# Linformer attention with a maxout FFN on one core: the last batch's softmax sums leave TensorE, and batch 0's first quarter of q is loaded as fp32

## The chip, the cores and the metric

The kernel runs on one core of one Trainium2 chip. The metric is the device time of one execution in microseconds (us). A profile of one execution, with a trace of every instruction and DMA packet, lies beside the times. In the trace PE is TensorE (PEld its weight loads), DVE is VectorE, ACT is ScalarE, POOL is GpSimd, and SP is the engine whose queue issues most DMAs.

## The reference, cut to what matters

```python
# q, k, v: (8, 8, 1024, 64) = batch, head, position, head_dim; E, F: (64, 1024)
k_proj = np.einsum('ks,bhsd->bhkd', E, k)          # 64 keys per head
v_proj = np.einsum('ks,bhsd->bhkd', F, v)
scores = scale * np.matmul(q, k_proj.transpose(0, 1, 3, 2))
attn = np.exp(scores - scores.max(-1, keepdims=True))
attn = attn / (attn.sum(-1, keepdims=True) + 1e-09)
attn_out = np.matmul(attn, v_proj)
x = attn_out.transpose(0, 2, 1, 3).reshape(8 * 1024, 512)
h = np.maximum(np.maximum(x @ w1, x @ w2), x @ w3)  # w1, w2, w3: (512, 768)
out = h @ w_out                                     # w_out: (768, 512)
```

All tensors are fp32 in memory. The kernel computes in bf16 with fp32 accumulation and takes the exponentials without subtracting the maximum.

## The kernel before, in words

**Stages.** The kernel works through eight batches. The FFN of batch b is the main stream: for each of two chunks (`ch`) of 512 positions there are six up steps (`up`, one per 128 columns of the hidden layer: 3 weight matrices times 4 contraction tiles, 12 matmuls of 512 columns) and four down steps (`down`, 6 matmuls of 512 columns for 128 positions). In an up step ACT copies the first product to SBUF (`h1s`), and VectorE takes two maxima (`m12`, then `hT`). In a down step of batches 1 to 7 ACT copies the result (`o_sb`), and every second down step a 512 KB store goes out on SP's queue.

**Order.** The order on every engine is written by hand: `tc.manual_schedule` keeps program order, and Tile adds the semaphores. The attention of batch b+1 is slipped in behind single steps of batch b's FFN. `plan(b)` (L830) is a table from (chunk, step) to functions, where steps 0 to 5 are the up steps and 6 to 9 the down steps; `behind` runs the entry after the step. PSUM banks are dealt by `bank` and `two` from a clock model (`runs`, `pe`, `free`) that is kept while the program is written; it sets which bank is used, not the order.

**Attention of a later batch.** `qd` packs q and turns it by DMA to `qT`; `kvproj` or `kproj`/`vproj` make the projected keys and values; `sc(b, g)` computes the scores of the head pair g with the keys on the partitions (two halves of the positions on partitions 0 to 63 and 64 to 127) and ACT writes their exponentials, the softmax numerators, as bf16 into `pTs[b, g, 0]`. `zc(b)` (L256) then sums the numerators of all four head pairs over the keys with eight matmuls against the constant `pick`, takes the reciprocal on ACT as exp(-ln), writes it to a DRAM scratch `zd`, and reads it back four times with a broadcast over 64 partitions into `zi_all`. `vx(b, g)` (L291) multiplies numerators by projected values on TensorE (`values`, four 64x64 tiles) and VectorE scales the product with `zi_all` into `xT`, the input of batch b's up steps. For the last batch, b = 7, `zc` stands behind up step 3 of chunk 0 of batch 6, and `vx` behind steps (1, 2) and (1, 6) of batch 6.

**The start.** E and F come on SP's queue (L148, L149). q, k, v and the weights of the start come on POOL's queue, which turns fp32 into bf16 on the way (`load_q`, `load_kv`, `load_w`); the first is q of heads 0 to 3 for the first half of each partition's positions (L167). Batch 0's first 512 positions are then worked off in an order of their own (L652 to L682): TensorE runs 512-column fp32 matmuls on zeros (`idle`) to stay busy, `turn_ef` casts E and F to bf16 on VectorE and ACT, turns them on TensorE and copies them to `efT`; `q_duo(0)` turns q with 16 transposes, and VectorE copies them to `qT`; then a VectorE copy doubles one part of `efT`, one more `idle`, and `k_duo(0)` (L593) projects the first four heads' keys.

Of the kernel before, what the change touches and what calls it, by code (L numbers as in the profile page):

```python
# [8 lines left out]
FP32 = mybir.dt.float32  # L9
BF16 = mybir.dt.bfloat16  # L10
AF = mybir.ActivationFunctionType
ALU = mybir.AluOpType
# [3 lines left out]
def kernel(  # L16
# [13 lines left out]
    nc = tc.nc  # L30

    B, H, S, D = q.shape
# [5 lines left out]
    P = 128  # L38
    HALF = 64
    SI = 8  # L40
    NCT = DM // P
    NJT = DF // P
    NPAIR = H // 2
    CHUNK = 512
    NCHUNK = S // CHUNK
    SPC = SI // NCHUNK
# [5 lines left out]
    att = ctx.enter_context(tc.tile_pool(name="att", bufs=2))  # L52
    scratch = ctx.enter_context(
        tc.tile_pool(name="scratch", bufs=2, space=bass.MemoryType.DRAM)
    )
# [21 lines left out]
    def two():  # L77
        n = min(range(0, 8, 2), key=lambda n: max(free[n:n + 2]))
        deal((n, n + 1))
        return psum_t[:, n:n + 2, :], (n, n + 1)  # L80

    def bank():
        n = min(range(8), key=lambda n: free[n])
        deal((n,))
        return psum_t[:, n, :], (n,)

    def pe(dt, wait=0.0):
        clock["pe"] = max(clock["pe"], wait) + dt
        return clock["pe"]

    def runs(eng, ready, dt, ns=()):
        if eng in clock:
            clock[eng] = max(clock[eng], ready + 0.06) + dt
            for n in ns:
                free[n] = clock[eng]
            return clock[eng]
        return ready + dt
# [3 lines left out]
    def copy(eng, o, i, ns=(), dt=0.65):  # L101
        done = {  # L102
            "v": nc.vector.tensor_copy, "s": nc.scalar.copy, "g": nc.gpsimd.tensor_copy
        }[eng](out=o, in_=i)
        runs(eng, clock["pe"] if ns else 0.0, dt, ns)
        return done
# [10 lines left out]
    def view(src, b):  # L117
        return src[b].rearrange("h (p si) d -> p h si d", si=SI)


    ident = const.tile([P, P], BF16, name="ident")
# [9 lines left out]
    qkv, qTs, kpTs, vps, pTs, zis, xTs = {}, {}, {}, {}, {}, {}, {}  # L131
# [24 lines left out]
    def load_q(heads, sis):  # L156
        nc.gpsimd.dma_start(
            out=q_t[:, heads, sis], in_=view(q, 0)[:, heads, sis]
        )
# [4 lines left out]

    LO, HI, ALL = slice(0, H // 2), slice(H // 2, H), slice(0, H)
    V2, V3 = slice(4, 6), slice(6, 8)
    load_q(LO, slice(0, SPC))  # L167
    load_kv(1, LO)
    load_q(HI, slice(0, SPC))
    load_kv(1, HI)  # L170
# [80 lines left out]
    def zi_all(b):  # L251
        if b not in zi_alls:
            zi_alls[b] = att.tile([P, NPAIR, 2, CHUNK], FP32, name="zi_all", bufs=1)
        return zi_alls[b]

    def zc(b, queue=nc.sync):  # L256
# [31 lines left out]
                zis[b, g, 0] = zi_all(b)[:, g], when  # L288
        return f

    def vx(b, g):  # L291
        def f():
            scale_x(b, g, 0, SI, values(b, g, 0, SI))
        return f
# [75 lines left out]

    q_pk = {}

    def pack_q(b, gs, lo, nsi):


        def f():
            if b not in q_pk:
                q_pk[b] = att.tile([P, NPAIR, SI, 2, D], BF16, name="q_p", bufs=1)
            for g in gs:
                copy(  # L380
                    "s", q_pk[b][:, g, lo:lo + nsi].rearrange("p si h d -> p h si d"),
                    qkv[b][0][:, 2 * g:2 * g + 2, lo:lo + nsi], (), 0.58,
                )
        return f

# [184 lines left out]
    def turn_ef():  # L570
        for i in range(2):
            cols = slice(i * S // 2, (i + 1) * S // 2)
            copy("vs"[i], ef_b[:, cols], ef_f[:, cols])
        t, ns = two()
        t = t.bitcast(BF16)[:, 0]
        src = ef_b.rearrange("k (p si) -> k p si", si=SI)
        for si in range(SI):
            nc.tensor.transpose(
                out=t[:, si * P:(si + 1) * P], in_=src[:, :, si], identity=ident
            )  # L580
        pe(0.6)
        for i in range(2):
            copy(
                "vs"[i], efT[:, 4 * i:4 * i + 4, 0:P],
                t[:, i * CHUNK:(i + 1) * CHUNK].rearrange("p (si x) -> p si x", x=P), ns,
            )
# [46 lines left out]
    def q_duo(u):  # L633
        t, ns = bank()
        t = t.bitcast(BF16)
        for gg in range(2):
            heads_q(0, 2 * u + gg, range(SPC), t[:, gg * CHUNK:(gg + 1) * CHUNK])
        o = qTs[0].rearrange("a (g si) p -> a g si p", si=SI)
        copy(
            "v", o[:, 2 * u:2 * u + 2, 0:SPC, :],  # L640
            t.rearrange("a (g si p) -> a g si p", si=SPC, p=P), ns, 0.7,
        )

    C0 = (0, SPC)

    def z(g):
# [5 lines left out]
    idle(3, warm_f)  # L652
    at(6.3)
    turn_ef()
    q_duo(0)
    copy("v", efT[:, :, P:P + KP], efT[:, :, KP:P])
    idle(1, warm_f)
    at(9.0)
# [22 lines left out]
    v_pair(1)  # L681
    at(17.4)  # L682

    ffn_sb = ctx.enter_context(tc.tile_pool(name="ffn_sb", bufs=2))
    hTs = {}

    def up_mm(h, i, b, ch, jt, cts, first=0, last=NCT - 1):
# [14 lines left out]
    def up_first(work):  # L702


        def then(key):
            run_later()
            for f in work.get(key, []):
                f()

        hs = ffn_sb.tile([P, NJT, CHUNK], FP32, name="hs", bufs=1)  # L710
        hTs[0, 0] = ffn_sb.tile([P, NJT, CHUNK], BF16, name="hT")
        jts = range(NJT)
        h = {}
        for ct, js in (
            (0, range(0, 4)), (1, range(0, 4)), (0, range(4, 6)), (1, range(4, 6)),
            (2, jts), (3, jts),
        ):
            for jt in js:
                if jt not in h:
                    t, ns = two()  # L720
                    for n in (0, 1):
                        h[jt + n] = t[:, n], ns[n:n + 1]
                up_mm(h[jt][0], 0, 0, 0, jt, (ct,))
                if ct == NCT - 1:
                    copy("sv"[jt % 2], hs[:, jt], *h[jt])
                then((0, ct, jt))
        for i in (1, 2):
            h = []
            for jt in jts:
                h.append(bank())  # L730
                up_mm(h[jt][0], i, 0, 0, jt, range(NCT // 2))
                then((i, "a", jt))
            for jt in jts:
                up_mm(h[jt][0], i, 0, 0, jt, range(NCT // 2, NCT))
                most(hs[:, jt] if i == 1 else hTs[0, 0][:, jt, :], *h[jt], hs[:, jt])
                then((i, jt))
# [93 lines left out]
    def plan(b):  # L830
        n = b + 1
        if b == 0:
            return {
                (0, 6): [
                    duo[1].sums, duo[1].values, duo[0].scale, duo[1].invert,
                ],
                (0, 7): [
                    qd(1, range(2)), duo[1].scale, qd(1, range(2, 4), "s"), store_now,
                ],
                (1, 1): [kproj(1)],  # L840
                (1, 2): [kt(1)],
                (1, 3): [sc(1, 0, now=True), sc(1, 1), vproj(1), ld(2)],
                (1, 4): [za(1, 0), sc(1, 2, now=True)],
                (1, 5): [za(1, 1)],
                (1, 6): [sc(1, 3, now=True)],
                (1, 7): [za(1, 2)],
                (1, 8): [za(1, 3)],
            }
        if b == 1:
            return {  # L850
                (0, 0): [qd(2)],
                (0, 3): [kproj(2), vproj(2), ld(3, (0,))],
                (0, 4): [kt(2)],
                (0, 5): [sc(2, 0, now=True), sc(2, 1, now=True), sc(2, 2)],
                (0, 6): [sc(2, 3, now=True)],
                (0, 8): [zc(2, nc.gpsimd), ld(3, (1, 2))],
                (1, 1): [qd(3)],
                (1, 3): [vx(2, 0), vx(2, 1)],
                (1, 6): [vx(2, 2), vx(2, 3)],
            }  # L860
        if b == 2:
            return {
                (0, 2): [kproj(3), vproj(3), ld(4)],
                (0, 3): [kt(3)],
                (0, 4): [sc(3, 0, now=True), sc(3, 1)],
                (0, 5): [sc(3, 2, now=True), sc(3, 3, now=True)],
                (0, 7): [zc(3)],
                (0, 8): [qd(4)],
                (1, 3): [kproj(4), vproj(4), ld(5), vx(3, 0), vx(3, 1)],
                (1, 4): [kt(4)],  # L870
                (1, 8): [vx(3, 2), vx(3, 3), sc(4, 0)],
            }
        if n == B:
            return {}
        out = {
            (0, 1): [sc(n, 1, now=True), sc(n, 2, now=True), sc(n, 3)],
            (0, 3): [zc(n)],
            (1, 2): [vx(n, 0), vx(n, 1)],
            (1, 6): [vx(n, 2), vx(n, 3)],
        }  # L880
        if n + 1 < B:
            out[0, 4] = [qd(n + 1)]
            out[1, 2] = [kvproj(n + 1)] + out[1, 2]
            out[1, 6] += [sc(n + 1, 0)]
        if n + 2 < B:
            out[1, 3] = [ld(n + 2)]
        return out
# [68 lines left out]
```

## Time and profile before

| | us |
|---|---|
| median of 9 executions | 399.34 (398.98 to 399.5) |
| profiled execution | 399.01 |
| its span in the trace | 397.2 |
| PE busy | 387.0 (97%) |
| PEld busy | 173.6 (44%) |
| DVE busy | 202.4 (51%) |
| ACT busy | 151.9 (38%) |
| POOL busy | 34.3 (9%) |

The span is the time from the first to the last instruction in the trace; 1.8 us of the profiled execution lie around it. The profiled execution is 0.33 us under the median. A line of a timeline gives start, duration, engine, line of the code, operation, output and inputs, count, and in brackets how long the engine sat idle before it and what ended that. "q0" in the view of the DMA queues is POOL's queue and "q1" is SP's.

### The profile page before, as it was taken

What the parts mean: (1) busy time and instruction counts of PE and PEld (TensorE: products, weight loads), DVE (VectorE), ACT (ScalarE), POOL (GpSimd) and SP (SyncE); (2) the same over time, 40 slices, a digit from 0 to 9 for tenths busy, and PEclk for the clock granted to TensorE, in tenths of its full rate; (3) what the DMA queues carried; (4) which work ended last, traced back from release to release, by engine and by line L of the source; (5) the groups of instructions that cost most, each with busy time, mean ns of one, the idle gap of its engine ahead of it and who ended that gap; (6) DMA issues with size and microseconds to landing.
All of it is one profiled execution on the core that took longest, in us unless ns stands there. A gap on an engine that the chain in (4) does not pass through costs nothing.

```text
span 397.2 us, 5598 instructions
## 1 busy us (share of the span) xinstructions
PE 387.0 (97%) x2196; PEld 173.6 (44%) x2238; DVE 202.4 (51%) x309; ACT 151.9 (38%) x236; POOL 34.3 (9%) x49
## 2 busy tenths in 40 slices
PE   7999999999999999999999999999999999999996
PEld 3444443453445445444444444444444444444443
DVE  3348756751764535645374544845266443745251
ACT  2534638527222552263323532245323533132322
POOL 7440001000400200200002000200000000000000
PEclk9999999999999999999999999999999999999999
DMA  9999999988999999999979969598971128020202
GB/s 152 205 205 207 205 230 155 245 153 166 233 180 257 151 227 211 219 179 208 211 208 149 246 144 252 117 233 147 220 210 42 63 85 238 2 106 0 107 0 106
DMA packets 67338, 66.29 MB, mean 167 GB/s; under 512 B 31504, under 2 KB 59792, under 8 KB 67312
## 3 DMA queue, kind: packets, MB, share of 16 engines
q0 software_dynamic: 29104, 30.41, 47.5%
q1 hardware_dynamic: 38064, 35.46, 34.9%
q8 instruction: 17, 0.28, 0.3%
q10 hardware_dynamic: 144, 0.07, 0.1%
q14 instruction: 9, 0.07, 0.1%
HBM read 69.73 MB, written 16.97 MB: 218 GB/s over the span
## 4 chain that ended last, share of the span: by engine, by line
PE 91%; DVE 2%; DMA 2%; ACT 2%; issue 2%; POOL 0%; DVEq 0%; ACTq 0%; POOLq 0%
PE banks L689 61%; PE banks L797 20%; PE banks L239 2%; PE banks L219 2%; PE banks L353 2%; DMA k_t<-in_k_dram 2%; PE banks L528 1%; DVE xT L316 1%; PE banks L264 1%; ACT zl L299 1%; DVE m L758 1%; ACT zi_all L305 1%; PE banks L596 1%; DVE hT L699 0%; PE banks L622 0%
## 5 line engine op out<-in xcount | busy, mean ns | idle before, releaser
L689 PE MATMUL banks<-xT,w_sb 128*128 128x512 bf16 x1125 | 255.2, 379 | 1.9 <-DVE xT L316 0.3
L689 PEld LDWEIGHTS <-w_sb 128*128 128x128 bf16 x1152 | 110.2, 98 | 136.7 <-issue 8.4
L758 DVE TENSOR_TENSOR m<-banks,h1s 128x512 f32<-128x512 f32 x90 | 62.1, 690 | 130.9 <-ACT h1s L754 88.2
L754 ACT COPY h1s<-banks 128x512 f32<-128x512 f32 x90 | 52.6, 585 | 119.6 <-PE banks L689 119.6
L797 PE MATMUL banks<-wout_sb,hT 128*128 128x512 bf16 x364 | 85.5, 380 | 1.0 <-issue 0.3
L699 DVE TENSOR_TENSOR hT<-banks,m 128x512 bf16<-128x512 f32 x90 | 62.3, 692 | 9.7 <-DVE m L758 0.5
L797 PEld LDWEIGHTS <-hT 128*128 128x128 bf16 x378 | 35.3, 98 | 48.3 <-issue 6.1
L102 ACT COPY o_sb<-banks 128x512 f32<-128x512 f32 (+2 forms) x57 | 32.9, 577 | 58.4 <-PE banks L797 50.6
L316 DVE TENSOR_TENSOR xT<-banks,zi_all 128x1024 bf16<-128x1024 f32 x28 | 33.1, 1219 | 12.8 <-PE banks L239 8.2
L230 ACT ACTIVATE pT<-banks 128x1024 bf16<-128x1024 f32 (+1 forms) x32 | 30.2, 975 | 15.8 <-PE banks L219 15.8
L201 POOL DMA_DIRECT2D q_t<-in_q_dram x7 | 6.1, 877 | 198.5 <-DMA kpT<-kp 42.3
L102 ACT CAST vp<-banks 64x256 bf16<-64x256 f32 (+1 forms) x11 | 4.7, 423 | 20.5 <-DVE kp L102 11.2
L102 DVE CAST vp<-banks 64x256 bf16<-64x256 f32 (+2 forms) x15 | 6.7, 444 | 10.4 <-ACT vp L102 7.2
L239 PE MATMUL banks<-pT,vp 64*64 64x512 bf16 (+1 forms) x128 | 10.3, 375 | 0.5 <-DVE vp L102 0.2
L102 DVE COPY q_p<-q_t 128x1024 bf16<-128x1024 bf16 x26 | 9.8, 437 | 0.6 <-DMA q_t<-in_q_dram 0.6
L219 PE MATMUL banks<-qT,kpT 64*64 64x512 bf16 (+1 forms) x128 | 9.7, 372 | 0.0
L102 DVE CAST kp<-banks 128x256 bf16<-128x256 f32 (+2 forms) x9 | 4.6, 509 | 8.4 <-PE banks L528 3.5
L102 DVE COPY o_sb<-banks 128x512 f32<-128x512 f32 (+1 forms) x9 | 5.6, 639 | 5.4 <-PE banks L777 4.5
L299 ACT ACTIVATE zl<-banks 128x512 f32<-128x512 f32 (+1 forms) x8 | 6.5, 810 | 2.9 <-PE banks L239 2.7
L353 PEld LDWEIGHTS <-efT 128*64 128x64 bf16 x128 | 6.6, 110 | 2.1 <-issue 2.1
L567 PE MATMUL banks<-warm_f 128*128 128x512 f32 x8 | 6.0, 890 | 1.5 <-DVE warm_f L175 1.5
L201 POOL DMA_DIRECT2D v_t<-in_v_dram x7 | 6.3, 900 | 1.0 <-PE banks L689 1.0
(76 smaller groups left out, 136.2 us busy)
## 6 DMA issues: line engine op xcount, KB each, us to landing
out_dram<-o_sb SPq DMA_DIRECT2D x30, 512.0 KB, 3.9
zi_all<-zd SPq DMA_DIRECT2D x20, 512.0 KB, 7.8
q_t<-in_q_dram POOLq DMA_DIRECT2D x7, 1024.0 KB, 10.7
k_t<-in_k_dram POOLq DMA_DIRECT2D x7, 1024.0 KB, 17.0
v_t<-in_v_dram POOLq DMA_DIRECT2D x7, 1024.0 KB, 22.2
zi_all<-zd POOLq DMA_DIRECT2D x4, 512.0 KB, 8.0
w_sb<-in_moe_w_dram POOLq DMA_DIRECT2D x4, 384.0 KB, 11.4
k_t<-in_k_dram POOLq DMA_DIRECT2D x2, 512.0 KB, 8.7
```

Of the source, the lines that this page charges most:

```text
L102: done = {"v": nc.vector.tensor_copy, "s": nc.scalar.copy, "g": nc.gpsimd.tensor_copy}[eng](out=o, in_=i)
L201: dma = nc.gpsimd.dma_start(out=tiles[i], in_=view((q, k, v)[i], b))
L219: nc.tensor.matmul(out=t[c * HALF:(c + 1) * HALF, hp, 0:n * P], lhsT=k_pair(b, g)[rows], rhs=qTs[b][rows, at:at + n, :], start=True, stop= ...
L230: nc.scalar.activation(out=pTs[b, g, lo], in_=t, func=AF.Exp, scale=scale)
L239: nc.tensor.matmul(out=t[hp * HALF:(hp + 1) * HALF, c, 0:nsi * HALF], lhsT=w(rows, hp), rhs=p[rows, hp, :], start=True, stop=True,)
L316: nc.vector.tensor_tensor(out=xTs[b][:, g, lo:lo + nsi, :].rearrange("a (c s) p -> a c (s p)", c=2), in0=t, in1=zi, op=ALU.mult,)
L353: nc.tensor.matmul(out=t[hh * HALF:(hh + 1) * HALF, 0:width], lhsT=efT[:, si, (kv - 1) * KP:kv * KP], rhs=qkv[b][kv][:, heads[hh], si, :], ...
L689: nc.tensor.matmul(out=h, lhsT=w_sb[i][:, ct, jt * P:(jt + 1) * P], rhs=xTs[b][:, ct, ch * SPC:(ch + 1) * SPC, :], start=(ct == first), st ...
L699: nc.vector.tensor_tensor(out=o, in0=h, in1=other, op=ALU.max)
L754: nc.scalar.copy(out=h1s, in_=h[0][0])
L758: nc.vector.tensor_tensor(out=m12, in0=h[1][0], in1=h1s, op=ALU.max)
L797: nc.tensor.matmul(out=o_ps, lhsT=hTs[b, ch][:, jt, tt * P:(tt + 1) * P], rhs=wout_sb[:, jt, :], start=(jt == 0), stop=(jt == NJT - 1),)
```

## The change

There are two edits.

**Last batch's sums.** For b = 7 alone `zc` goes. Behind up step (0, 2) of batch 6 four DMA transposes on SP's queue (`turn_p`, 128x1024 bf16 each) turn the numerators, so that positions lie on the partitions and keys along the row. Behind the down steps (0, 8) and (0, 9) VectorE sums over the keys with four `tensor_reduce` of 1024 elements per partition (`sum_p`), takes the reciprocal of 64 columns and transposes it in 32x32 blocks (`spread_z`). Two DMAs write that to `zd`, and the four broadcasts to `zi_all` follow as before. `vx` moves from (1, 2) to (1, 5) and from (1, 6) to (1, 8).

**First q.** The load of q for heads 0 to 3 leaves POOL's queue. It becomes the third DMA on SP's queue, behind E and F, and brings fp32 into the buffer `hs`, which otherwise holds intermediate maxima of up_first. In `turn_ef`, between the casts of E and F and the copies of `efT`, VectorE and ACT each cast one head pair to bf16 into the packed tile `q_p` (`pack_q`). `q_first` turns it with eight 128x128 transposes instead of `q_duo(0)`'s sixteen of 128x64.

```diff
--- before.py
+++ after.py
@@ -164,7 +164,12 @@
     LO, HI, ALL = slice(0, H // 2), slice(H // 2, H), slice(0, H)
     V2, V3 = slice(4, 6), slice(6, 8)
-    load_q(LO, slice(0, SPC))
+    ffn_sb = ctx.enter_context(tc.tile_pool(name="ffn_sb", bufs=2))
+    hs = ffn_sb.tile([P, NJT, CHUNK], FP32, name="hs", bufs=1)
+    q_f = hs[:, 0:2].rearrange("p j f -> p (j f)").rearrange(
+        "p (h si d) -> p h si d", h=H // 2, d=D
+    )
+    nc.sync.dma_start(out=q_f, in_=view(q, 0)[:, LO, 0:SPC])
     load_kv(1, LO)
     load_q(HI, slice(0, SPC))
     load_kv(1, HI)
@@ -288,6 +293,65 @@
                 zis[b, g, 0] = zi_all(b)[:, g], when
         return f
+    s_T, p_T = {}, {}
+    def turn_p(b, g):
+        def f():
+            if b not in s_T:
+                s_T[b] = att.tile([P, NPAIR, 2, SPC, 2], FP32, name="s_T")
+            p_T[b, g] = att.tile([P, 2, CHUNK // 2], FP32, name="zi0", bufs=4).rearrange(
+                "p a f -> p (a f)"
+            ).bitcast(BF16).rearrange("p (n x) -> p n x", x=P)
+            nc.sync.dma_start_transpose(
+                out=p_T[b, g], in_=pTs[b, g, 0].rearrange("p h f -> p (h f)")
+            )
+        return f
+    def sum_p(b, g):
+        def f():
+            nc.vector.tensor_reduce(
+                out=s_T[b][:, g].rearrange("p h s c -> p (h s) c"),
+                in_=p_T[b, g].rearrange("p n (c k) -> p n c k", c=2),
+                axis=mybir.AxisListType.X, op=ALU.add,
+            )
+            runs("v", 0.0, 1.15)
+        return f
+    def spread_z(b, queue=nc.sync):
+        def f():
+            n = NPAIR * 4 * SPC
+            zr = att.tile([P, n], FP32, name="zr")
+            nc.vector.reciprocal(
+                out=zr.rearrange("p (a c s) -> p a c s", c=2, s=SPC),
+                in_=s_T[b].rearrange("p g h s c -> p (g h) c s"),
+            )
+            zt = att.tile([P, n], FP32, name="zt")
+            nc.vector.transpose(out=zt, in_=zr)
+            when = runs("v", 0.0, 0.35) + 11.0
+            zd = scratch.tile([NPAIR, 2, 2, CHUNK], FP32, name="zd")
+            rows = zd.rearrange("g h c (s a r) -> (g h c s) a r", a=4, r=32)
+            for j in range(2):
+                nc.sync.dma_start(
+                    out=rows[32 * j:32 * (j + 1)].rearrange("i a r -> a i r"),
+                    in_=zt[:, 32 * j:32 * (j + 1)],
+                )
+            for u in range(2):
+                gs = slice(2 * u, 2 * u + 2)
+                for hp in range(2):
+                    queue.dma_start(
+                        out=zi_all(b)[hp * HALF:(hp + 1) * HALF, gs],
+                        in_=zd[gs, hp].partition_broadcast(HALF),
+                    )
+            for g in range(NPAIR):
+                zis[b, g, 0] = zi_all(b)[:, g], when
+        return f
     def vx(b, g):
         def f():
             scale_x(b, g, 0, SI, values(b, g, 0, SI))
@@ -370,16 +434,17 @@
     q_pk = {}
-    def pack_q(b, gs, lo, nsi):
+    def pack_q(b, gs, lo, nsi, engs="ss", src=None):
         def f():
             if b not in q_pk:
                 q_pk[b] = att.tile([P, NPAIR, SI, 2, D], BF16, name="q_p", bufs=1)
-            for g in gs:
+            for g, eng in zip(gs, engs):
+                i = qkv[b][0][:, :, lo:lo + nsi] if src is None else src
                 copy(
-                    "s", q_pk[b][:, g, lo:lo + nsi].rearrange("p si h d -> p h si d"),
-                    qkv[b][0][:, 2 * g:2 * g + 2, lo:lo + nsi], (), 0.58,
+                    eng, q_pk[b][:, g, lo:lo + nsi].rearrange("p si h d -> p h si d"),
+                    i[:, 2 * g:2 * g + 2], (), 0.58,
                 )
         return f
@@ -571,6 +636,7 @@
         for i in range(2):
             cols = slice(i * S // 2, (i + 1) * S // 2)
             copy("vs"[i], ef_b[:, cols], ef_f[:, cols])
+        pack_q(0, (0, 1), 0, SPC, "vs", q_f)()
         t, ns = two()
         t = t.bitcast(BF16)[:, 0]
         src = ef_b.rearrange("k (p si) -> k p si", si=SI)
@@ -641,6 +707,24 @@
             t.rearrange("a (g si p) -> a g si p", si=SPC, p=P), ns, 0.7,
         )
+    def q_first():
+        t, ns = bank()
+        t = t.bitcast(BF16)
+        for gg in range(2):
+            for si in range(SPC):
+                n = gg * SPC + si
+                nc.tensor.transpose(
+                    out=t[:, n * P:(n + 1) * P],
+                    in_=q_pk[0][:, gg, si].rearrange("p h d -> p (h d)"),
+                    identity=ident,
+                )
+        pe(0.5)
+        o = qTs[0].rearrange("a (g si) p -> a g si p", si=SI)
+        copy(
+            "v", o[:, 0:2, 0:SPC, :],
+            t.rearrange("a (g si p) -> a g si p", si=SPC, p=P), ns, 0.7,
+        )
     C0 = (0, SPC)
     def z(g):
@@ -652,7 +736,7 @@
     idle(3, warm_f)
     at(6.3)
     turn_ef()
-    q_duo(0)
+    q_first()
     copy("v", efT[:, :, P:P + KP], efT[:, :, KP:P])
     idle(1, warm_f)
     at(9.0)
@@ -681,7 +765,6 @@
     v_pair(1)
     at(17.4)
-    ffn_sb = ctx.enter_context(tc.tile_pool(name="ffn_sb", bufs=2))
     hTs = {}
     def up_mm(h, i, b, ch, jt, cts, first=0, last=NCT - 1):
@@ -707,7 +790,6 @@
             for f in work.get(key, []):
                 f()
-        hs = ffn_sb.tile([P, NJT, CHUNK], FP32, name="hs", bufs=1)
         hTs[0, 0] = ffn_sb.tile([P, NJT, CHUNK], BF16, name="hT")
         jts = range(NJT)
         h = {}
@@ -878,6 +960,13 @@
             (1, 2): [vx(n, 0), vx(n, 1)],
             (1, 6): [vx(n, 2), vx(n, 3)],
         }
+        if n + 1 == B:
+            del out[0, 3]
+            out[0, 2] = [turn_p(n, g) for g in range(NPAIR)]
+            out[0, 8] = [sum_p(n, 0), sum_p(n, 1)]
+            out[0, 9] = [sum_p(n, 2), sum_p(n, 3), spread_z(n)]
+            out[1, 5] = out.pop((1, 2))
+            out[1, 8] = out.pop((1, 6))
         if n + 1 < B:
             out[0, 4] = [qd(n + 1)]
             out[1, 2] = [kvproj(n + 1)] + out[1, 2]
```

## The prediction

> **What bounds the kernel now.** I read the page's chain of waits first, then the chain of the first 26 us, then the timelines at the two places that the diff touches. The page's chain by engine says that the end is TensorE's own work:
>
> ```profile
> PE 91%; DVE 2%; DMA 2%; ACT 2%; issue 2%; POOL 0%; DVEq 0%; ACTq 0%; POOLq 0%
> ```
>
> So there are two ways to move the end: take TensorE work out of a full stretch, or change the few microseconds in which TensorE waits. The 2% of DMA are one piece, at the start (chain in order of time; start, length, what):
>
> ```profile
> 1.26 0.88 POOL q_t L157
> 2.14 7.46 DMA k_t<-in_k_dram
> 9.60 0.04 issue
> 9.64 1.03 PE banks L596 x8
> ```
>
> The first keys land at 9.60, and `k_duo(0)` starts at 9.64. After that the chain names no DMA again: ACT, VectorE and TensorE hand on to each other until TensorE is full at about 21 us. A delay of `k_duo(0)` therefore reaches the end whole. A gain does not: the second keys release a POOL load at 13.77 and TensorE takes them at 13.85, so less than 0.1 us can be won unless the whole load stream moves too.
>
> What stands in front of the keys on TensorE and VectorE (timeline):
>
> ```profile
> 6.49 0.65 PE L578 MATMUL banks<-ident,ef_b 128*128 128x128 bf16 x8 [0.19 <-POOL ident masks.py:199]
> 7.07 0.64 PE L364 MATMUL banks<-ident,q_t 128*64 128x128 bf16 x16
> 7.63 1.12 PE L567 MATMUL banks<-warm_f 128*128 128x512 f32 x2
> 7.75 0.69 DVE L102 COPY qT<-banks 128x1024 bf16<-128x1024 bf16 x1
> 8.36 0.28 DVE L102 COPY efT<-efT 128x512 bf16<-128x512 bf16 x1
> ```
>
> q is there before 7.07, and everything in front of `k_duo(0)` is over at 8.75. The cover in front of the keys is 0.9 us and no more.
>
> At the last batch's place (timeline of batch 6):
>
> ```profile
> 319.14 0.61 PE L264 MATMUL banks<-pT,pick 128*32 128x512 bf16 x8
> 319.68 4.86 PEld L689 LDWEIGHTS <-w_sb 128*128 128x128 bf16 x24 [0.42 <-issue]
> ...
> 346.04 0.96 PEld L797 LDWEIGHTS <-hT 128*128 128x128 bf16 x5
> ...
> 347.21 0.10 PEld L797 LDWEIGHTS <-hT 128*128 128x128 bf16 x1 [0.20 <-DVE hT L699]
> ```
>
> TensorE is full on both sides of L264. The last line is the sixth matmul of the first down step, 0.20 us late because VectorE's last `hT` is.
>
> **What the Trainium skill says.** "DMA: Bandwidth & Descriptors", section Queues, rings and completion order: each DMA engine takes turns, packet by packet, among the queues that have work. The trace agrees, and sharply. With a DMA transpose and a load both waiting, 119 to 120 us:
>
> ```profile
> q0 software_dynamic: 155, 0.16, 93.0%
> q1 hardware_dynamic: 153, 0.04, 29.6%
> ```
>
> 155 packets against 153, though the bytes differ by four to one. The same page, section SWDGE vs HWDGE vs iDMA: only POOL's queue casts on the way; hence the fp32 buffer and the two new casts. "VectorE: DVE Perf Modes", section The perf-mode tier table: `tensor_reduce` runs one element per cycle at any type; "TensorE: Matmul & The Clock Gate", Part 1: the array falls to half its clock after an idle window of about 3.4 us. The trace shows a slow start, its first fp32 matmuls (L567) at 1061 ns and later ones at 592, but no drop after an idle stretch, since none is that long.
>
> **Part 1, the last batch's sums.** Removed: `zc`. 24 up matmuls start at 313.85; at 0.216 each (36 of them take 7.78 us from 338.48 to 346.26) they are through at 319.03, but the next one starts at 319.69. So `zc` costs TensorE **0.66 us**, all on the path. Its Ln and Exp on ACT (0.60, 0.63) lie beside TensorE: nothing. Moved: `vx` costs TensorE the same wherever it stands, and each pair 2.35 us of VectorE. At (1, 5) eight value matmuls (0.55) come between the last up step and the first down step and cover the 0.20 wait: **0.20 us** more, 0 if a bank is not free. At (1, 8) VectorE is done 2.82 us after the values start (347.64 to 350.46 in the old place); the next batch's fourth contraction tile is wanted after 0.55 + 1.30 (a down step) + 1.94 (nine matmuls) = 3.8 us, the third after 2.3 and ready after 1.7. Nothing waits.
>
> Added, all behind cover. SP: a transpose of 4096 columns occupies it for 10.95 us (279.28), so one of 1024 takes 2.74. The exponentials end at 316.9 at the latest; SP, free from 309, issues the last transpose by about 322.7, landed near 325. Behind it on SP waits only a store that is ready at 328.3. VectorE: 1024/0.96 GHz and overhead, 1.1 to 1.2 us each as an estimate from the skill; the trace's one-rate operations on 1024 columns (L316) take 1.22. Four, and two small operations of some 0.2, make 5.2 us from 325.8 to 331.0; VectorE's next due work is at 333.03. Then two `zd` DMAs (issue 0.54 each, landing 1.8 to 2.8) and four broadcasts (issue 0.60, landing 5.1 to 10.2): all landed by about 346.5. The first two, which (1, 5) needs at 347, come near 341; the others are wanted at 351. The DMA engines are 21% to 45% busy here. Sum of part 1: **-0.86 us**, bounds -1.0 and 0.
>
> **Part 2, the first q.** Bytes read do not change: E, F, q and k are there when the keys are, before and after. What changes is the order. Before, q goes ahead of the keys in one queue. Now q is behind F in SP's queue and the keys head POOL's, and the engines take turns. Both transfers have 512 packets (four heads times 128 partitions), 32 per engine. In the stretch from 4 to 6 us POOL's queue comes into its own as SP's ends:
>
> ```profile
> q0 software_dynamic: 547, 0.29, 114.6%
> q1 hardware_dynamic: 37, 0.09, 17.8%
> ```
>
> and in 2 to 4 us it has moved 3 packets. So q's packets and the keys' start together at about 4, alternate, and **finish together**. Keys and q took until 9.6 in sequence, and the same work interleaved ends at the same time: q lands near 9.5 where it was there by 7.07. Upper bound 10.2 (F's last bytes move before 5, yet its casts start at 5.66: SP's landings lag); lower bound 8.3, if SP, which issues q at about 2.0 and needs 1.4 from issue to first byte (E: 0.74 to 2.1), gets half a microsecond ahead while F's slow reads leave gaps.
>
> From the landing: casts of 512 columns on VectorE and ACT, 0.67 with the wait (`ef_b` took 0.61 and 0.62); eight transposes start 0.1 later, and the copy to `qT` follows after 0.55 (eight take 0.5). On VectorE the `efT` copy (0.43) fits in between, but it too is now held behind the cast, as ACT's is. Then 0.69 for `qT`, 0.28 for the doubling, 0.05: `k_duo(0)` starts **2.37 us after the landing**. TensorE gives the same: transposes 0.5, `idle` 0.85 to 1.1. At 9.5 that is 11.87 against 9.64: **+2.2 us**, bounds +1.0 (8.3) and +2.9 (10.2). Everything on TensorE is queued behind the transposes. POOL's queue wins one issue (0.89 us), worth nothing: its data wait for the engines, which are busy from 2 us on, and the ninth load and those after it wait for landings as before. The eight transposes saved (0.2 us) are off the path now that q is late.
>
> **Sum.** 399.01 - 0.86 + 2.2 = 400.35 for the profiled execution; set on the median, which is 0.33 higher, 400.7.
>
> **The rivals.** (a) As summed, q lands between 8.9 and 10.2: 399.34 - 0.86 + 1.65 to 2.9 = 400.1 to 401.4. Chance 0.60.
> (b) Not slower: q hides. One mechanism: SP's queue runs ahead of POOL's. E reaches the engines 1.4 us after its issue, while POOL's first data need 2.7 (1.26 to 4.0); if 16 of q's 32 packets per engine pass in that gap, q lands near 7.3 and `k_duo(0)` waits for the keys as before. For: POOL's lag. Against: F's bytes stand in front until after 4. It decides below a landing of 8.9, where the delay (1.65) less 0.86 is under 0.8; 398.5 at best, 399.3 at 8.1. Chance 0.22.
> (c) As (a), and the clock falls. TensorE has no plain matmul from 6.3 to the second `idle` near 11: 4.7 us. If an idle window falls in it, `idle` and `k_duo(0)` take twice their 0.85 each and part of what follows too: +1.5 on (a), 402.2. For: the slow start in the trace. Against: the window must fall right and the transposes may count. Chance 0.13.
> (d) Part 1 fails: a bank or a broadcast is late at (1, 5) and TensorE waits; nothing saved and up to 1 us lost, 401.5 to 402.5. Five microseconds of margin speak against it. Chance 0.05.
>
> **The numbers.** 400.7 is the middle of (a). The range 398.9 to 402.5 takes in most of (b) and (c). A measurement of this kernel tells about 0.2% (0.8 us) from no change. Slower by more is most of (a), (c), (d) : 0.71; within it the edge of (a) and most of (b): 0.22; faster by more than that, a landing before 7.3: 0.07.
>
> **What would show it.** Right: the chain at the start runs through q's landing at SP's queue, a cast and transposes, and no longer through `k_t`; `k_duo(0)` near 11.9; POOL's and SP's packets alternate from 4 us on; TensorE's wait for the casts grows to about 3 us. In batch 6 the up matmuls run on without the 0.66 gap, the 0.20 wait at the first down step is gone, and the reductions take about 1.2 each, over before VectorE's next maximum. Wrong: q landing before 8, the fp32 matmuls of the second `idle` at 1061 ns, or a wait of `xT` at the values or the next batch's first up step.

## The result, and the profile after

| | us |
|---|---|
| median before (31 executions) | 399.22 (398.44 to 399.77) |
| median after (10 executions) | 402.86 (402.23 to 404.96) |
| ratio | 1.0104, 95% interval 1.0093 to 1.0114 |
| profiled execution after | 404.12, span 402.3 |

The changed kernel is 3.6 us slower. 400.7 was predicted with a range of 398.9 to 402.5: the direction was right, the median is 2.2 us above the forecast, and the range missed it by 0.4 us. The span grew by 5.1 us in the profiled execution, which lies among the longer ones, and by less in most.

The chain in order of time in the changed kernel (start, length, what) shows the place:

```profile
2.01 10.31 DMA hs<-in_q_dram
12.32 0.02 issue
12.35 0.44 DVE q_p L102
12.78 0.05 issue
12.83 1.03 PE banks L716 x8
13.87 1.81 PE banks L632 x2
15.68 1.48 PE banks L662 x8
```

It runs as the prediction's list of signs had it: q on SP's queue, a cast, the transposes (L716), the second `idle` (L632), `k_duo(0)` (L662). But q lands at 12.32 instead of 9.5, and in the timeline `k_duo(0)` comes at 15.61 instead of 11.87. There, what TensorE and VectorE waited for:

```profile
6.92 0.71 PE L644 MATMUL banks<-ident,ef_b 128*128 128x128 bf16 x8 [0.17 <-ACT ef_b L102]
12.35 0.43 DVE L102 CAST q_p<-hs 128x512 bf16<-128x512 f32 x1 [5.66 <-DMA hs<-in_q_dram]
12.83 1.03 PE L716 MATMUL banks<-ident,q_p 128*128 128x128 bf16 x8 [5.20 <-DVE q_p L102]
```

TensorE stands still for 5.2 us. The page shows what that does to its clock; the second slice of forty is 10 to 20 us:

```profile
PEclk9699999999999999999999999999999999999999
```

The batch 6 part went as forecast. Three lines of its timeline:

```profile
319.69 10.53 PE L772 MATMUL banks<-xT,w_sb 128*128 128x512 bf16 x47
330.86 4.59 DVE L315 TENSOR_REDUCE s_T<-zi 128x16 f32<-128x1024 bf16 x4
335.02 15.42 PEld L772 LDWEIGHTS <-w_sb 128*128 128x128 bf16 x72
```

The up matmuls of steps 2 to 5 run on without the eight of `pick`. From the start of step 2 to the next chunk's first weight load it takes 335.02 - 319.68 = 15.34 us, where it took 329.84 - 313.85 = 15.99 before: **0.65 us** saved. The reductions end at 335.45, well before VectorE's next maximum at 338.21.

### The profile page after: what moved, and what is told of

It is laid out like the page before. It is cut to its first block, busy times and chain, and to the rows that moved or that the text cites. A ratio compares the mean times of both kernels' runs of the same rounds, so it can differ in the third digit from the quotient of the medians.

```text
span 402.3 us, 5580 instructions
## 1 busy us (share of the span) xinstructions
PE 388.5 (97%) x2180; PEld 174.4 (43%) x2222; DVE 207.9 (52%) x316; ACT 151.3 (38%) x235; POOL 33.6 (8%) x48
## 4 chain that ended last, share of the span: by engine, by line
PE 91%; DMA 3%; DVE 3%; issue 1%; ACT 1%; SPq 0%; DVEq 0%; ACTq 0%
PE banks L772 60%; PE banks L879 19%; DMA hs<-in_q_dram 3%; PE banks L244 2%; PE banks L224 2%; PE banks L417 2%; PE banks L593 1%; DVE xT L380 1%; PE banks L632 1%; PE banks L269 1%; PE banks L662 1%; ACT zi_all L369 1%; ACT zl L363 1%; DVE m L840 0%; DVE hT L782 0%
## 5 line engine op out<-in xcount | busy, mean ns | idle before, releaser
L102 ACT CAST vp<-banks 64x256 bf16<-64x256 f32 (+1 forms) x11 | 4.7, 424 | 20.5 <-DVE kp L102 11.2
L244 PE MATMUL banks<-pT,vp 64*64 64x512 bf16 (+1 forms) x128 | 10.3, 375 | 0.2 <-DVE vp L102 0.2
L632 PE MATMUL banks<-warm_f 128*128 128x512 f32 x8 | 7.3, 1069 | 1.5 <-DVE warm_f L180 1.5
## 6 DMA issues: line engine op xcount, KB each, us to landing
q_t<-in_q_dram POOLq DMA_DIRECT2D x7, 1024.0 KB, 10.2
w_sb<-in_moe_w_dram POOLq DMA_DIRECT2D x4, 384.0 KB, 10.3
```

The lines of the kernel that those rows point to most:

```text
L102: done = {"v": nc.vector.tensor_copy, "s": nc.scalar.copy, "g": nc.gpsimd.tensor_copy}[eng](out=o, in_=i)
L244: nc.tensor.matmul(out=t[hp * HALF:(hp + 1) * HALF, c, 0:nsi * HALF], lhsT=w(rows, hp), rhs=p[rows, hp, :], start=True, stop=True,)
```

## The experiments

Two theories of q's late landing were set against each other. **A**: a transfer of SP's or ACT's queue starts late when POOL's queue pours packets into the DMA engines first. **B**: 512 small packets, or the third place on SP's queue, take that long by themselves. Every ratio below is against executions of the kernel before that were taken with the run.

**The sums alone** (`sums_only`):

```diff
-    nc.sync.dma_start(out=q_f, in_=view(q, 0)[:, LO, 0:SPC])
+    load_q(LO, slice(0, SPC))
...
-        pack_q(0, (0, 1), 0, SPC, "vs", q_f)()
...
-    q_first()
+    q_duo(0)
```

> The last batch's sums alone; q comes as before. Both theories of the start expect the same: TensorE loses the 0.66 us of the eight matmuls against pick and keeps everything else. 399.22 - 0.65 = 398.6 us, ratio 0.998 to 0.9985. The 0.20 us that the prediction gave to the wait of the first down step is not expected: in the changed kernel that stretch takes as long as before. If instead 398.3 or less, the wait was worth something.

Measured: 398.08 us, ratio 0.9975 (0.9966 to 0.9983). The sums alone are a gain of 0.7 to 1.4 us; the part that the trace can place is again 0.65, between steps (0, 2) and (0, 6) of batch 6 (328.93 - 313.59 = 15.34 us). The median is under the 398.3 that was named as a sign that the wait at the first down step was worth something, but the trace does not bear that out: from the second chunk's first weight load to the next batch's it takes 350.98 - 328.93 = 22.05 us, and 22.04 in the kernel before. What else the median gained is not explained; in the profiled execution 0.26 us of it lies ahead of this stretch and about 0.2 behind it.

**The first q alone** (`q_only`): the changed kernel without the `if n + 1 == B:` block of `plan`.

> The first q as fp32 on SP's queue alone; the last batch's sums as before. Both theories of the start: the whole loss and the 0.65 us that the sums no longer give back, 402.86 + 0.65 = 403.5 us (ratio 1.010 to 1.013). Less than 402.9 would mean that the two edits disturb each other.

Measured: 403.2 us, ratio 1.0103 (1.0090 to 1.0116). All of the loss is here. q landed at 11.38. The two edits do not add up cleanly: the two ratios multiply to 1.0078, and the changed kernel has 1.0104. q's landing varies from execution to execution, but whether that makes the difference was not measured.

**q from ACT's queue** (`q_act`):

```diff
-    nc.sync.dma_start(out=q_f, in_=view(q, 0)[:, LO, 0:SPC])
+    nc.scalar.dma_start(out=q_f, in_=view(q, 0)[:, LO, 0:SPC])
```

> The changed kernel with the fp32 q issued from ACT's queue, ahead of its table load, at about 0.7 us instead of 2.0. Theory A (a transfer of SP's or ACT's queue starts late when POOL's queue has filled the engines first): q starts near 2.1 beside E, is through before the keys' packets come at 4, and lands at 5 to 6; TensorE waits for the keys at 9.6 as in the kernel before; 398 to 398.9 us. Theory B (512 small packets take their queue 4 us and more to begin and 8 to 10 to make): q lands at 9 to 11 and the time is 401 to 402.5. A third reading (the engines share bandwidth by packet, nothing else): q lands near 7.5, 398.5 to 399.

Measured: 399.55 us, ratio 1.0004 (0.9992 to 1.0015). q was issued at 0.74 and landed 4.7 us later. The view of the DMA queues for 2 to 4 us (q10 is ACT's queue, q1 SP's; packets, MB, share):

```profile
q10 hardware_dynamic: 515, 0.52, 76.4%
q1 hardware_dynamic: 31, 0.13, 21.3%
```

Nearly all of q's packets pass in two microseconds. The first half of B falls: 512 packets are quick when nothing of POOL is there. So does the third reading, since q landed at 5.4 and not near 7.5. The order works the other way too: POOL's queue, whose keys came in behind, passed 15 packets from 4 to 6 us, against 244 in the changed kernel.

The median misses A's window by 0.65 us, and the executions fall into two groups. Ten show a granted clock of 0.999 or 1.0, and their median of 398.2 is inside the window; twelve show 0.991 to 0.996, with a median of 399.85. The profiled one, at 398.75, is of the first group. In it F is late: from 2 to 4 us q holds the engines and SP's queue passes 31 packets, where it passed 123 in the kernel before, and the last of F meets POOL's packets. F lands at 7.80, after 6.42 us where it took 4.2 before, and `k_duo(0)` comes at 10.55:

```profile
1.38 6.42 DMA ef_f<-in_F_dram
```

TensorE was idle for 1.61 us ahead of the turn of E and F and kept its clock. That it waits longer in the other twelve is likely but was not traced.

**q first on SP's queue** (`q_sp_first`): the two DMAs of E and F moved behind q's.

> The changed kernel with the fp32 q issued first on SP's queue and E and F behind it. Theory A: q's packets start near 2.1 and are mostly through by 4.5; E and F, now the ones that meet POOL's packets, land at 8 to 10 instead of 4.5 and 6.2, and the first key matmul comes at 11.5 to 13: 400 to 402 us. Theory B: q lands at 9 or later though it is first, and E and F behind it later than that: 403 us or more.

Measured: 402.75 us, ratio 1.0089 (1.0076 to 1.0102). q landed 4.3 us after its issue, at 5.0; F, issued at 1.90, landed at 9.34. As A has it, what is issued last is late; but E and F also stood behind q's 512 packets in their own queue, and this run does not tell the two apart. The time is above A's window, since `k_duo(0)` came only at 13.77: after 3.7 us without work TensorE's clock had fallen here too (0.991 over the execution, and 2.02 us for the two fp32 matmuls of the second `idle`).

**The keys held until q is there** (`keys_held`):

```diff
-    nc.sync.dma_start(out=q_f, in_=view(q, 0)[:, LO, 0:SPC])
-    load_kv(1, LO)
+    q_dma = nc.sync.dma_start(out=q_f, in_=view(q, 0)[:, LO, 0:SPC])
+    after(nc.gpsimd.dma_start(out=qkv[0][1][:, LO], in_=view(k, 0)[:, LO]), q_dma)
```

> The changed kernel with POOL's first key load, and all POOL loads behind it, held until the fp32 q has landed. Theory A (POOL's packets get ahead of a transfer of SP that is issued while they pour in): without them q, still third on SP's queue and issued at 2.0, lands at 6 to 6.8 instead of 12.3. If it still lands at 9 or later, its place behind E and F on SP's queue is the cause and not POOL. The keys then land at 12 to 13 and the whole load stream is 4 to 5 us late, so the time says little: 402 to 404.5 us.

Measured: 403.45 us, ratio 1.0112 (1.0099 to 1.0125). q is still third on SP's queue and issued at 2.01. Its line in the chain:

```profile
2.01 4.74 DMA hs<-in_q_dram
```

4.74 us instead of 10.31, with nothing changed but POOL's packets. In the traces q's first packet passes at 3.9 us instead of 6.2, and the 512 take 2.3 us instead of 5.8. The second half of B falls and A stands, in two parts: beside POOL's packets q starts later, and it shares the engines for longer. (POOL also makes the identity matrix after its first loads, so holding POOL held the turn of E and F to 11.47; the time is not a price of the keys alone.)

**TensorE kept busy** (`warm`): `idle(5, warm_f)` ahead of `q_first()`.

> The changed kernel with five more fp32 matmuls on zeros of 0.85 us each between the turn of E and F and the turn of q, where TensorE stands idle. If the clock that falls in this gap is part of the loss, the granted clock stays at 1.0, the second idle takes 1.1 us instead of 2.0 and the first key matmuls 1.03 instead of 1.55, and the time falls by 1.0 to 1.5 us to 401.4 to 401.9. If the loss is q's landing alone: 402.6 to 403.

Measured: 402.0 us, ratio 1.0072 (1.0060 to 1.0084) against the changed kernel's 1.0104: about 1 us of the loss goes with the clock (0.9 by the medians, 1.3 by the ratios). The median is 0.1 us above the expected window. The clock was held: 0.998 to 1.0 in all five executions. The fp32 matmuls of the second `idle`, first in the changed kernel and then here (ns, shortest, median, longest):

```profile
L632 PE MATMUL banks<-warm_f x2: 1061/1114/1167, 13.7 to 14.6; 128*128 128x512 f32 x2
```

```profile
L632 PE MATMUL banks<-warm_f x2: 592/620/648, 12.5 to 13.0; 128*128 128x512 f32 x2
```

With the clock held, the transposes of q begin at 12.03, as the added matmuls end, and `k_duo(0)` follows 1.45 us later, at 13.48. In the changed kernel it is 2.78 us later (12.83 to 15.61). The 1 us is not a clean price of the clock: q landed at 11.2 here, 1.1 us earlier than in the profiled execution of the changed kernel, and the first weight load of q's transposes was over by 11.78, so the added matmuls themselves held the transposes for about 0.3 us.

**The keys ahead of q** (`keys_first`): `pack_q` taken out of `turn_ef`, and with `q_first` put behind `kt_duo(0)`, ahead of the first scores.

```diff
     kt_duo(0)
     idle(1)
+    pack_q(0, (0, 1), 0, SPC, "vs", q_f)()
+    q_first()
```

> The changed kernel with the casts and the turn of q moved behind the first keys' projection and transposes, in front of the first scores. If what costs is that everything on TensorE, VectorE and ACT is queued behind q, the first key matmul is back at 9.6 to 10 us, and q holds up the scores alone: landing at 11.4 to 12.3, scores 2 us later against 11.7 in the kernel before, of which 0.66 us is absorbed: 399.5 to 401 us. If q's lateness costs the same wherever it is waited for: 402.5 or more.

Measured: 398.97 us, ratio 0.9998 (0.9990 to 1.0006), better than expected. The chain:

```profile
2.01 8.45 DMA hs<-in_q_dram
...
11.63 0.70 DVE qT L102
12.34 0.04 issue
```

q still lands at 10.46, nearly as late, and holds up the scores to 12.38 against 11.73 in the kernel before. But the first keys land at 8.4, are projected and turned while q is on its way, and TensorE keeps its clock (0.999 to 1.0 in all executions). Most of the loss was work queued behind q that did not need q, with the clock that fell meanwhile. Not all of it is gone: `sums_only`, which differs in q alone, has a ratio of 0.9975, so q on SP's queue still costs about 0.9 us here.

**The sums for more batches**: `n + 1 == B` in `plan` becomes `n + 2 >= B` (`sums_67`) and `n + 3 >= B` (`sums_567`), with q as before; the next batch's first scores move with `vx`.

> q as in the kernel before, and the sums by DMA and VectorE for batches 6 and 7. If the saving is the eight matmuls per batch and nothing waits, twice 0.65 us: 397.4 us, ratio 0.9955 to 0.9965. Against it: in batch 5 SP's queue also turns q of batch 7 (11 us of issue) and batch 6's transposes stand in front of it; if the sums then come late for the values at step (1, 5), 398.5 us or more.

Measured: 397.6 us, ratio 0.9964 (0.9951 to 0.9976). This is the fastest version; its ratio says 1.4 us less than before, not surely more than the sums of one batch give.

> q as in the kernel before; sums by DMA and VectorE for batches 5, 6 and 7. Batch 4 carries loads on POOL's queue that the later ones lack. If a transfer of SP's queue starts 3 to 5 us late beside loads, as q did, four transposes, two writes and four broadcasts in a row for batch 5 come too late for the values at step (1, 5), and the third batch gives nothing or loses: 397.6 us or more. If the margin holds, a further 0.65 us: 396.9 to 397.1.

Measured: 399.93 us, ratio 1.0026 (1.0011 to 1.0040): the third batch costs more than all three save. SP's four transposes for batch 6 now occupy its queue from 262.54 for 22.2 us beside the loads (17.1 from 262.92 in `sums_67`, 9.6 in the changed kernel's quiet batch 6), and what follows on that queue slips. The waits of 294 to 316 us (who waited for whom, total, times, longest):

```profile
DVE xT L380 <- DMA zi_all<-zd: 2.9, 1, 2.9
...
PE banks L224 <- DMA kpT<-kp: 2.1, 1, 2.1
```

The scores of batch 7 wait for its turned keys, which share the queue with the sums. Neither wait is there in `sums_67`.

## Why the prediction was wrong

**Part 1, the sums.** Right in mechanism and cover, 0.65 against 0.86. The term that was mis-sized is the 0.20 us for the wait at the first down step: the profile shows it as idle time of the weight load, and TensorE lost nothing by it. From the second chunk's first weight load to the next batch's it is 357.07 - 335.02 = 22.05 us with the wait gone and was 351.88 - 329.84 = 22.04 with it.

**Part 2, where q lands.** The step that failed is "q's packets and the keys' start together at about 4", and with it "finish together" and the upper bound of 10.2. From 4 to 6 us in the changed kernel SP's queue passes 37 packets, as many as before without q, and POOL's has the engines nearly to itself:

```profile
q0 software_dynamic: 244, 0.25, 85.2%
q1 hardware_dynamic: 37, 0.09, 15.8%
```

q's first packet passes at 6.2. From 6 to 8 us:

```profile
q0 software_dynamic: 280, 0.26, 82.8%
q1 hardware_dynamic: 150, 0.15, 27.4%
```

and from 8 to 10, when they do alternate:

```profile
q0 software_dynamic: 349, 0.20, 67.9%
q1 hardware_dynamic: 309, 0.31, 56.0%
```

Once under way, q took 5.8 us, close to the 5.5 (4 to 9.5) that the prediction gave it: the sharing was sized about right, and the start was 2.2 us off. The rest of the 2.8 us is 0.3 for the longer passage, at the end of which SP's queue passed only 24 packets from 10.5 to 12 us, and 0.4 from the last packet to the landing. The keys had the engines nearly alone for their first microseconds and came a little earlier than before (8.4 in `keys_first`, 9.3 in the changed kernel, against 9.6); q shared with what stood behind them, and landed at 10.5 to 12.3 in the four executions traced. That is rival (b) turned round: not SP ahead of POOL, but POOL ahead of SP. It could have been read in the kernel before. On SP's queue, beside loads and in the quiet batch 6, the same 32 KB write to `zd`, and the broadcasts that wait for it:

```profile
181.93 0.54 SPq L276 DMA_DIRECT2D zd<-zic  x1
186.58 2.55 SPq L283 DMA_DIRECT2D zi_all<-zd  x4
```

```profile
321.09 0.54 SPq L276 DMA_DIRECT2D zd<-zic  x1
322.96 2.55 SPq L283 DMA_DIRECT2D zi_all<-zd  x4
```

4.7 us from one to the other beside loads, 1.9 without. I priced a moved transfer by bandwidth and a start of 1.4 us that was measured when nothing else was under way. The turn-taking that the Trainium skill states ("DMA: Bandwidth & Descriptors", Queues, rings and completion order) fits the stretch from 8 to 10 us and not the one before it; whether q's packets had not reached the engines by then, or were there and got no turn, no view tells.

**From the landing to the keys.** 2.37 us was set for a full clock, 0.77 of it up to the transposes and 1.60 after. Measured were 3.29 (12.32 to 15.61): 0.51 up to the transposes, since VectorE's cast took 0.43 and not 0.61, and 2.78 after them, where `warm` needed 1.45. The clock had fallen. Rival (c) happened as well, with a chance of 0.13 set on it. All eleven executions of the changed kernel, the profiled one with them, show a granted clock of 0.987 to 0.996, where the profiled one of the kernel before shows 1.0 and the others on record 0.998 to 1.0. The chance was set for a gap that the early landing had made short; with q at 12.3 the gap is 5.2 us. The Trainium skill ("TensorE: Matmul & The Clock Gate", Part 1) names an idle window of about 3.4 us: the traces agree, with 1061 to 1167 ns a matmul after the gap of 5.2 us, 1061 to 1163 after 3.7 us in `q_sp_first`, and 592 to 648 after 1.61 us in `q_act` and without a gap in `warm`.

**"A delay reaches the end whole".** Not quite: 0.65 us was absorbed. The first up matmul of batch 0 is 6.49 us later than before (23.81 against 17.32), the first after the third value projection 5.84 (26.79 against 20.95, in the chain). Before, that projection waited:

```profile
20.33 0.45 PEld L622 LDWEIGHTS <-efT 128*128 128x128 bf16 x8 [0.92 <-DMA v_t<-in_v_dram]
```

In the changed kernel v has long landed and the same weight load (L688, 25.97) waits for nothing. The chain before named ACT at this point, whose release fell within 0.1 us of v's; but in the changed kernel the projection starts at 26.18 while the same piece of work on ACT (`zi`, 26.15 to 26.78) is still running, so it was v that held it.

**The sum for the profiled execution.** Predicted for `k_duo(0)` 2.23; q's landing 2.82 more; 0.92 more from the landing to the keys (0.26 less up to the transposes, 1.18 more after them at the fallen clock); together 5.97, as measured. Then 0.52 for `k_duo(0)` and its followers at the slow clock, less 0.65 absorbed, less 0.65 of part 1: 5.19, against 5.1 in the spans. The median execution is 1.3 us shorter than the profiled one; q's landing varies by 1.9 us among the profiles, and how the shorter ones divide between landing and clock was not measured.

**What stays open.** Why packets of SP's queue pass late beside POOL's is not shown; the experiments show that POOL's packets are the cause and not q's shape or its place on SP's queue. How much of the loss is the clock alone is not separated from how long TensorE waits.

## What to carry to other kernels

Before moving a transfer from one queue to another, look up how long that queue's own transfers take to land beside the same load, not in a quiet stretch, and issue early what must land early. When data may come late, put the code that needs it behind the code that does not: the late q cost about 4.1 us at the head of the work of three engines (`q_only`) and about 0.9 behind the keys. Taking a reduction from a full TensorE to a VectorE with room to spare gave back its matmuls here, 0.65 of 0.66 us, as long as what follows on the DMA queue that carries it still came in time.

## What the runs showed of the hardware

- A 512 KB transfer of 512 packets landed 4.3 to 4.7 us after its issue when it was ahead of POOL's packets or without them, and 8.5 to 10.3 us after it when it was issued beside them.
- After 5.2 us without work TensorE's fp32 matmuls of 512 columns took 1061 to 1167 ns instead of 592 to 648, and keeping it busy through the gap gave back about 1 us.
- VectorE reduced 1024 bf16 columns to 16 in 1.21 us, as the prediction's row had it; a reciprocal of 64 fp32 columns took 0.55, more than the 0.2 that was set for each of two small operations.
